# A fused convolution, MLP and top-1 expert kernel: the expert tiles as 89 of 256 tokens and 21 of 128, the first expert's weights queued ahead of its rows, and a second buffer for dispatched rows

## The chip, the cores and the metric

The kernel runs on one core of a Trainium2 chip. The metric is the device time of one launch in microseconds. Lower is better. The engines are called here as the profile calls them: PE multiplies matrices (its weight loads stand apart, as PEld), DVE and ACT do elementwise work, POOL does elementwise work and issues indirect DMAs, and SP issues nearly all other DMAs.

## The reference

Three blocks follow each other over 8 sequences of 3072 tokens of width 256, 24576 tokens in all: a long convolution by FFT, a dense MLP, and a layer of 8 experts in which each token goes to the one expert of its largest logit.

```python
def _attn_ref(x, filt_r, filt_i):
    X = np.fft.rfft(x, axis=1)
    F = (filt_r + 1j * filt_i)[None, :, :]
    return np.fft.irfft(X * F, n=x.shape[1], axis=1).astype(np.float32)

def _moe_ref(x, w_in, w_out):                      # 256 -> 2048 -> 256
    h = x @ w_in
    g = np.where(h > 0.0, h, np.exp(np.minimum(h, 0.0)) - 1.0)
    return (g @ w_out).astype(np.float32)

def _moe2_ref(x, w_gate, w1, w2):                  # 8 experts, 256 -> 1024 -> 256
    ...
    expert_idx = np.argmax(logits, axis=1)
    ...
    for e in range(E):
        mask = expert_idx == e
        ...
        h = np.maximum(x[mask] @ w1[e], 0.0)
        out[mask] = gate_w[mask, None] * (h @ w2[e])
```

## The kernel before

All matrix products stand for fp32: each operand is split into a high and a low f16 part, and each product is done in three passes (`PASSES`: high by high, high by low, low by high).

After a first stage (transforms of the first sequence, conversion of the weights) one long loop in `stream` runs 768 MLP steps. A step takes 256 tokens and 256 of the 2048 hidden units: 12 up matmuls of 256 columns (L1037), tanh and exp on ACT, two operations on DVE (L1044, L1045, they write `th`, of which there are 3 buffers), the split into `g` on ACT and POOL, and, `LAG` = 5 steps later, 12 down matmuls of 264 columns (L1066), 8 of which are the expert logits. All other work is strewn between the steps: the transforms of later sequences (L626 is one of their products), the conversion of the expert weights into a scratch tensor `wscr`, and the dispatch of tokens. A planner (`chain`) puts each small piece at a step where the engine loads allow it; within an engine the order so found is fixed.

**Dispatch.** `dispatch_steps` works on a group of three tiles of 512 tokens, 16 groups in all. After routing, the `rows` steps run once per tile. `s5` takes a `row` buffer, POOL writes two columns of it (L782, L784), ACT the high parts (a line of a helper, L167) and DVE the low parts (L170). Four `s6` steps then scatter 128 rows each by indirect DMA on POOL (L793) into the DRAM tensor `srt`, sorted by expert. All these scatters write one tensor, so each waits until the one before it has landed. There is one `row` buffer: the next tile's `s5` waits until the last scatter of the tile before has read it.

**Experts.** Behind the 768 steps and `LAG` more come the expert steps. Since the counts of the experts are known only at run time, there are `nmoe` = 103 tiles of 256 tokens, which is enough for any counts; which expert a tile takes and where its rows begin is read from tables (`table_steps`). The first table, of `EARLY` = 8 tiles, is made while the last group of tokens is still in the MLP; the second, of the other 95, when all counts are known. `pads` (L1164) then writes zero rows behind each expert's end, in POOL's order after 8 of the last group's 12 scatters. A tile is 8 steps. Each has 6 up matmuls of 256 columns (L1206), relu and split on ACT (L1209) and DVE (L1210), and, `XLAG` = 4 steps later, 6 down matmuls of 256 columns (L1225). After the last step of a tile ACT scales the two results into `eo` (L1230, 12 buffers) and POOL scatters them to the output (L1231).

**The queue of SP.** `expert_rows` loads a tile's rows by DMA transpose (`xT`, L1183, 8 buffers) and its gates and positions (`me`, L1185). `expert_weights` loads 1 MB of `w1` or `w2` (L1194) if the tile's expert differs from that of the tile two before; tiles use two weight buffers by turns. The first 8 tiles' rows are issued first, then the weights of tiles 0 and 1. From tile 5 on, the end of tile i issues the rows of tile i + `XROWS` = i + 3, so the rows of tile 8, the first that need the second table, all scatters and all pads, are issued when tile 5 ends, and SP waits there until these have landed.

In what follows w10, w20 are the two weight buffers of tile 0, w11, w21 those of tile 1.

Of the kernel before, what the change touches and what calls it, by code (L numbers as in the profile page):

```python
# [101 lines left out]
TE = 256  # L102
ROW = 516
# [6 lines left out]
EARLY = 8  # L110
# [5 lines left out]
class Kernel:  # L116
    def __init__(self, ctx, tc, a, nb):
# [4 lines left out]
        self.nmoe = self.ntok // TE + E - 1  # L122
# [241 lines left out]
    def expert_weight_steps(self, sb, psum_tile):  # L364
# [339 lines left out]
    def dispatch_steps(self, sb, psum_tile, g):  # L704
# [202 lines left out]
    def stream(self, ctx, fft, sf, sy, ps, psum_tile, yt):  # L907

        nc, tc, nb = self.nc, self.tc, self.nb
        with tc.tile_pool(name="mlp", bufs=1, reuse_waits="tile") as sb:  # L910
# [112 lines left out]
            for k in range(min(plan), nstep + LAG + 8 * self.nmoe + XLAG):  # L1023
# [55 lines left out]
    def table_steps(self, early):  # L1079


        nc, n = self.nc, EARLY if early else self.nmoe - EARLY
        st = {}

        def s1():
            sb = self.xb
            if early:
                self.kt = self.t(sb, [1, 2 * E + 2 * self.nmoe], F32, "kt", 1)
                nc.sync.dma_start(self.kt, self.a["k_tab"])
            else:  # L1090
# [5 lines left out]
        def s2():  # L1096
# [16 lines left out]
        def s4():  # L1113
            cf = st["cf"]
            nc.vector.tensor_scalar(out=cf[:, 3, :], in0=cf[:, 1, :], scalar1=-float(TE), scalar2=float(self.cap), op0=ALU.mult, op1=ALU.add)
            if early:
                self.done = d = self.t(self.xb, [1, E], F32, "done", 1)
                nc.vector.tensor_tensor(out=d, in0=cf[:, 1, :], in1=cf[:, 2, :], op=ALU.subtract)
                nc.vector.tensor_scalar(out=d, in0=d, scalar1=float(EARLY), scalar2=0.0, op0=ALU.add, op1=ALU.max)
                nc.vector.tensor_tensor(out=d, in0=d, in1=cf[:, 1, :], op=ALU.min)  # L1120
            else:
# [175 lines left out]
```

## Time and profile before

| | before |
|---|---|
| median of 3 runs | 3755.59 us (3749.76 to 3758.88) |
| the profiled execution | 3759.05 us |
| its span, first to last instruction | 3757.4 us |
| mean granted clock of TensorE in it | 0.971 |
| PE busy | 3515.3 us, 94% of the span |
| DVE, ACT, POOL busy | 2537.5, 2450.1, 1677.4 us |

The rows are read as follows. Times are microseconds from the start of the span. In the timeline a row is a run of like instructions: its start, its length, engine, line, operation, output<-input, shapes, count, and in brackets how long the engine stood idle before it and what ended that. "a*b" in a matmul is the size of the weights, "a x b" that of the moving data; the matmuls are pipelined, so the time between two starts tells the cost, and the printed lengths overlap. PEclk 1.00 is a granted clock of 2.4 GHz, half of it 1.2 GHz.

### The profile page before, as it was taken

How to read it: one execution, taken by the hardware profiler on the slowest of the kernel's cores; microseconds unless marked ns; L12 is line 12 of the kernel's file. 1: busy time of each engine (PE TensorE's matmuls, PEld its weight loads, DVE VectorE, ACT ScalarE, POOL GpSimd, SP SyncE). 2: the span in 40 equal slices, each digit the busy share in tenths (PEclk: the TensorE clock that was granted, in tenths of full speed). 3: DMA queues.
4: the chain of work that ended last, by engine and by line, in shares of the span. 5: the costliest groups of instructions: out<-in, count | busy, mean ns of one | idle time of the engine just before them, and what ended most of it. 6: DMA issues, size and time to landing. Idle time of an engine off the chain costs nothing. (4 is left out here: it accounts for less than half of the span.)

```text
span 3757.4 us, 83940 instructions
## 1 busy us (share of the span) xinstructions
PE 3515.3 (94%) x31644; PEld 3048.6 (81%) x31644; DVE 2537.5 (68%) x4684; ACT 2450.1 (65%) x4556; POOL 1677.4 (45%) x1554
## 2 busy tenths in 40 slices
PE   3599899999999999999999999999799999999998
PEld 1377788888888888788888888888688888888887
DVE  4788779979988987987997986766333333333332
ACT  2486788888788788788788788777233333333333
POOL 1434447646655655655664665555221111111111
PEclk7689999999999999999999999999899999999999
DMA  7725324334333433433433422101332332333231
GB/s 227 217 87 157 97 83 142 102 95 132 102 107 103 120 105 101 130 91 97 137 93 90 119 84 79 49 18 33 95 102 52 93 87 60 96 96 85 63 94 35
DMA packets 313610, 371.65 MB, mean 99 GB/s; under 512 B 162558, under 2 KB 236544, under 8 KB 307714
## 3 DMA queue, kind: packets, MB, share of 16 engines
q1 hardware_dynamic: 292226, 312.28, 30.6%
q0 software_dynamic: 19360, 52.67, 4.2%
q8 instruction: 248, 4.06, 0.5%
q10 hardware_dynamic: 1616, 1.32, 0.2%
q14 instruction: 160, 1.31, 0.1%
HBM read 404.01 MB, written 123.44 MB: 140 GB/s over the span
## 5 line engine op out<-in xcount | busy, mean ns | idle before, releaser
L1051 POOL TENSOR_TENSOR g<-th,g 128x512 f16<-128x512 f32 x768 | 899.0, 1171 | 878.4 <-ACT g L167 800.9
L1037 PE MATMUL up<-yh,w_in 128*128 128x256 f16 x9216 | 1147.0, 275 | 35.1 <-DVE th L1045 32.1
L1066 PE MATMUL dn<-w_out,g 128*128 128x264 f16 x9216 | 1153.9, 277 | 9.4 <-ACT x L1073 9.4
L1037 PEld LDWEIGHTS <-w_in 128*128 128x128 f16 x9216 | 902.7, 99 | 179.5 <-issue 46.7
L1066 PEld LDWEIGHTS <-g 128*128 128x128 f16 x9216 | 905.9, 98 | 145.0 <-issue 9.7
L1210 DVE SCALAR_TENSOR_TENSOR hh<-up,hh 128x256 f16<-128x256 f32 x824 | 349.6, 425 | 711.2 <-ACT hh L1209 689.9
L1209 ACT ACTIVATE hh<-up 128x256 f16<-128x256 f32 x824 | 316.1, 384 | 685.5 <-PE up L1206 648.3
L1044 DVE SCALAR_TENSOR_TENSOR th<-ex,yS,th 128x512 f32<-128x512 f32 x768 | 574.3, 748 | 232.7 <-ACT ex L1043 208.4
L1206 PE MATMUL up<-xT,w 128*128 128x256 f16 x4944 | 677.7, 274 | 26.0 <-DVE hh L1210 17.1
L1043 ACT ACTIVATE ex<-up,yS,yI 128x512 f32<-128x512 f32 x768 | 574.3, 748 | 152.7 <-DVE th L1044 150.8
L1042 ACT ACTIVATE th<-up,yI 128x512 f32<-128x512 f32 x768 | 524.8, 683 | 208.7 <-PE up L1037 175.9
L1045 DVE SCALAR_TENSOR_TENSOR th<-th,up 128x512 f32<-128x512 f32 x768 | 528.6, 688 | 87.0 <-DVE th L1044 2.8
L1231 POOL DMA_INDIRECT out<-eo,me x206 | 202.2, 982 | 829.3 <-ACT eo L1230 486.1
L1206 PEld LDWEIGHTS <-w 128*128 128x128 f16 x4944 | 485.3, 98 | 84.5 <-issue 17.5
L1225 PEld LDWEIGHTS <-hh 128*128 128x128 f16 x4944 | 485.0, 98 | 57.1
L167 ACT ACTIVATE g<-th 128x512 f16<-128x512 f32 x768 | 483.4, 629 | 11.1 <-DVE th L1045 2.5
L1225 PE MATMUL dn<-w,hh 128*128 128x256 f16 x2496 | 342.0, 274 | 0.0
L1225 PE MATMUL ff<-w,hh 128*128 128x256 f16 x2448 | 333.9, 273 | 0.0
L793 POOL DMA_INDIRECT srt<-row,pi x192 | 198.0, 1031 | 144.2 <-DMA srt<-row,pi 119.4
L560 POOL TENSOR_TENSOR t<-t,t 128x512 f32<-128x512 f32 x96 | 124.8, 1300 | 48.6 <-DVE t L554 35.3
L554 DVE SCALAR_TENSOR_TENSOR t<-ff,fs,ft 64x512 f32<-64x512 f32 (+1 forms) x186 | 130.8, 709 | 2.5
L579 PEld LDWEIGHTS <-e 128*128 128x128 f16 x648 | 66.5, 105 | 76.0 <-issue 35.2
(266 smaller groups left out, 2781.2 us busy)
## 6 DMA issues: line engine op xcount, KB each, us to landing
w<-wscr SPq DMA_DIRECT2D x103, 1024.5 KB
w<-wscr SPq DMA_DIRECT2D x103, 1024.0 KB
ft<-filt SPq DMA_DIRECT2D x96, 512.0 KB
at<-ascr SPq DMA_DIRECT2D x192, 128.0 KB
bscr<-bst SPq DMA_DIRECT2D x192, 128.0 KB
bt<-bscr SPq DMA_DIRECT2D x64, 384.0 KB
x<-x SPq DMA_DIRECT2D x84, 256.0 KB
x<-x SPq DMA_DIRECT2D x112, 192.0 KB
```

Source lines behind the costliest of these rows:

```text
L167: self.nc.scalar.activation(out, in_, AF.Copy, scale=scale)
L1037: nc.tensor.matmul(p[:, c * TH:(c + 1) * TH], self.w_in[:, w, d, ff:ff + 128], h[:, m, d, c0:c0 + TH], start=(i == 0), stop=(i == 5))
L1042: nc.scalar.activation(th, p, AF.Tanh, scale=I[:, 1:2])
L1043: nc.scalar.activation(e, p, AF.Exp, bias=S[:, 2:3], scale=I[:, 0:1])
L1044: nc.vector.scalar_tensor_tensor(out=th, in0=e, scalar=S[:, 1:2], in1=th, op0=ALU.add, op1=ALU.mult)
L1045: nc.vector.scalar_tensor_tensor(out=th, in0=th, scalar=0.0, in1=p, op0=ALU.min, op1=ALU.max)
L1051: nc.gpsimd.tensor_tensor(out=g[:, 1, :], in0=th, in1=g[:, 0, :], op=ALU.subtract)
L1066: nc.tensor.matmul(dn[s][:, 0:D + E], g[:, m, c * TH + s * 128:c * TH + s * 128 + 128], self.w_out[:, 2 * f + c, w, :], start=(f == 0 and ...
L1206: nc.tensor.matmul(p, w1[:, w0:w0 + 128], xT[:, 2 * m + d, :], start=(q == 0), stop=(q == 5))
L1209: nc.scalar.activation(h[:, 0, :], p, AF.Relu)
L1210: nc.vector.scalar_tensor_tensor(out=h[:, 1, :], in0=p, scalar=0.0, in1=h[:, 0, :], op0=ALU.max, op1=ALU.subtract)
L1225: nc.tensor.matmul(self.xd[s], h[:, m, s * 128:(s + 1) * 128], w2[:, w0:w0 + D], start=(f == 0 and q == 0), stop=(f == 7 and q == 2))
```

## The change

- **Tiles.** 89 full tiles of 256 tokens and 21 parts of 128 tokens take the place of 103 full tiles. The full tiles cover what is certain to fill them; a third table gives each part its expert and place. A part stands after about every fourth full tile, from the tenth on. It has 4 steps; each has two chunks of 6 up matmuls with 128 columns, the same work for ACT and DVE as before, and 6 down matmuls of 256 columns. Parts use a third pair of weight buffers, one `xP` and two `mP` buffers for their rows, and are loaded when the part before has ended.
- **Buffers.** `row` 1 to 2; `wst` 3 to 2 (raw weights in conversion, with two more of the MLP's raw blocks in `ft`), `eo` 12 to 6, `xT` and `me` 8 to 7 (`EARLY` 8 to 7, so tile 7 is now the first that needs the second table, and its rows are issued when tile 4 ends).
- **SP's queue.** The four weight loads of tiles 0 and 1 are issued first, then the rows of tiles 0 to 6.
- **Tables and pads.** Each table gets one or two more short steps; the pads come after all three tables.

In the changed kernel the lines are some 3 further down in the first part (row scatter L796, `th` L1047 and L1048), and in the expert part: rows L1207, `me` L1209, weights L1218, up L1236, down L1260, output L1266, pads L1181.

The diff, cut to its core:

```diff
-EARLY = 8
+EARLY = 7
...
-        self.nmoe = self.ntok // TE + E - 1
+
+        self.nmoe = -(-(self.ntok - E * (TE - 1)) // TE)
+        self.npart = (self.ntok + E * (TP - 1)) // TP - 2 * self.nmoe
...
-            t = self.t(sb, [128, 1024], F32, "wst", 3)
+            t = self.t(sb, [128, 1024], F32, "wst", 2)
...
-                st["ri", i] = ri = self.t(sb, [128, 4, ROW // 2], I32, "row", 1)
+                st["ri", i] = ri = self.t(sb, [128, 4, ROW // 2], I32, "row", 2)
...
-                    pool, tag, n = (sf, "ft", 2) if 3 <= c < 5 else (sb, "wst", 3)
+                    pool, tag, n = (sf, "ft", 2) if c % 4 > 1 else (sb, "wst", 2)
...
-            ke = chain(ke, self.table_steps(True), kd[last + 1] + 8)
-            ke = max(ke, ks[last] + 8) + 1
+            ke = chain(ke, self.table_steps(0), kd[last + 1] + 8)
+            ke = max(ke, ks[last] + 2) + 1
+            for i in range(2):
+                at(ke + i, lambda i=i: (self.expert_weights(0, i, 0), self.expert_weights(0, i, 1)), ZERO)
             for i in range(EARLY):
-                at(ke + i // 2, lambda i=i: self.expert_rows(i), ZERO)
-            for i in range(2):
-                at(ke + 5 + i, lambda i=i: (self.expert_weights(i, 0), self.expert_weights(i, 1)), ZERO)
-            assert ke + 6 < nstep + LAG
-            kt = chain(kd[ng - 1], self.table_steps(False))
+                at(ke + 2 + i // 2, lambda i=i: self.expert_rows(0, i), ZERO)
+            assert ke + 6 < nstep + LAG, (ke, nstep)
+            kt = chain(chain(kd[ng - 1], self.table_steps(1)), self.table_steps(2))
             at(kt, self.pads, ZERO)
...
+        nc, n = self.nc, (EARLY, self.nmoe - EARLY, self.npart)[kind]
...
+        def s4b():
+            cf = st["cf"]
+            d = self.t(self.xb, [1, E], F32, "done", 2)
+            nc.vector.tensor_tensor(out=d, in0=cf[:, 1, :], in1=cf[:, 2, :], op=ALU.subtract)
+            nc.vector.tensor_scalar(out=d, in0=d, scalar1=float(n), scalar2=0.0, op0=ALU.add, op1=ALU.max)
+            nc.vector.tensor_tensor(out=d, in0=d, in1=cf[:, 1, :], op=ALU.min)
+            if kind:
+                nc.vector.tensor_tensor(out=d, in0=d, in1=self.done, op=ALU.add)
+            self.done = d
...
-        big = 0.1 if early else 1.0
-        return [((c, 0.0, 0.0), 1, f) for c, f in ((0.2, s1), (0.8, s2), (1.0, s3), (0.7, s4), (2 * big, s5), (2 * big, s6), (0.8, s7))]
+            self.tab[kind] = tab
+
+        big = 1.0 if kind == 1 else 0.2
+        steps = [(0.4, s1), (0.8, s2), (0.8, s3), (0.8, s4)] + ([(0.5, s4b)] if kind < 2 else []) + [(2 * big, s5), (2 * big, s6), (0.8, s7), (0.7, s8)]
+        return [((c, 0.0, 0.0), 1, f) for c, f in steps]
...
-        self.w1 = [self.t(sb, [128, 4096], F16, f"w1{i}", 1) for i in range(2)]
-        self.w2 = [self.t(sb, [128, 4098], F16, f"w2{i}", 1) for i in range(2)]
+        self.w1 = [self.t(sb, [128, 4096], F16, f"w1{i}", 1) for i in range(3)]
+        self.w2 = [self.t(sb, [128, 4098], F16, f"w2{i}", 1) for i in range(3)]
...
+        at, m = {}, self.nmoe - EARLY
+        for h in range(self.npart):
+            at.setdefault(EARLY + (h + 1) * m // (self.npart + 1), []).append((1, h))
+        self.order = [v for i in range(self.nmoe) for v in [(0, i)] + at.get(i, [])]
+        self.xsteps = [(part, i, f) for part, i in self.order for f in range(4 if part else 8)]
...
+        xT = self.t(sb, [128, 4, n], F16, "xP" if part else "xT", 1 if part else EARLY)
+        nc.sync.dma_start_transpose(xT, self.srt[bass.ds(r, n), 0:D].bitcast(F16))
+        me = self.t(sb, [128, n // 128, 2], I32, "mP" if part else "me", 2 if part else EARLY)
...
-        self.nc.sync.dma_start(dst[i % 2], src[:, c0:c1], cond=(g > 0), cond_hint=False)
+        self.nc.sync.dma_start(dst[2 if part else i % 2], src[:, c0:c1], cond=(g > 0), cond_hint=False)
...
+            part, i, f = self.xsteps[k]
+            if not part and i == EARLY and f == 0:
+                self.expert_rows(1, 0)
+                self.expert_weights(1, 0, 0)
+                self.expert_weights(1, 0, 1)
+            w1, (xT, _) = self.w1[2 if part else i % 2], self.tile_x[part, i]
+            n, nf = (TP, 2) if part else (TE, 1)
             p = self.t(ps, [128, 512], F32, "up", 3)[:, 0:TE]
-            q = 0
-            for w, m in PASSES:
-                for d in range(2):
-                    w0 = w * 2048 + d * 1024 + f * 128
-                    nc.tensor.matmul(p, w1[:, w0:w0 + 128], xT[:, 2 * m + d, :], start=(q == 0), stop=(q == 5))
-                    q += 1
+            for c in range(nf):
+                q = 0
+                for w, m in PASSES:
+                    for d in range(2):
+                        w0 = w * 2048 + d * 1024 + (f * nf + c) * 128
+                        nc.tensor.matmul(p[:, c * n:(c + 1) * n], w1[:, w0:w0 + 128], xT[:, 2 * m + d, :], start=(q == 0), stop=(q == 5))
+                        q += 1
...
+            if f == 8 // nf - 1:
+                self.expert_weights(part, i + (1 if part else 2), 0)
...
+            for s in range(n // 128):
+                for c in range(nf):
+                    for q, (m, w) in enumerate(PASSES):
+                        w0 = w * 2048 + (f * nf + c) * D
+                        h0 = (s + c) * 128
+                        nc.tensor.matmul(self.xd[s], h[:, m, h0:h0 + 128], w2[:, w0:w0 + D], start=(f == 0 and c == 0 and q == 0), stop=(f == last and c == nf - 1 and q == 2))
...
-                    o = self.t(sb, [128, D], F32, "eo", 12)
+                for s in range(n // 128):
+                    o = self.t(sb, [128, D], F32, "eo", 6)
...
+                self.expert_weights(part, i + (1 if part else 2), 1)
+                if part:
+                    self.expert_rows(1, i + 1)
+                elif i + XROWS >= EARLY:
+                    self.expert_rows(0, i + XROWS)
```

On SP, the first loads of the expert stage (TENSOR_LOAD reads a table entry, ISA rows are register work). Before:

```order
L1089 DMA kt_36235<-k_tab 1x222 [waits DMAHW7_49]
L1175 TENSOR_LOAD tab_5422_36512 [waits DVE_49]
L1175 ISA x2
L1183 ISA
L1183 DMA_TRANSPOSE xT_36591<-srt 128x4x256 [waits DMAHW0_49,DMASW3_49]
L1185 ISA
L1185 DMA me_36593<-srt 128x2x2 [waits DMAHW1_49,PE_49]
L1175 TENSOR_LOAD tab_5422_36512
...
L1194 DMA w_4964_33056<-wscr 128x4096 [waits DMAHW0_49]
```

and in the changed kernel:

```order
L1198 TENSOR_LOAD tab_5432_36582 [waits DVE_49]
...
L1218 DMA w_4964_33056<-wscr 128x4096 [waits DMAHW5_49,DMAHW6_49,DMAHW0_49,PE_49]
...
L1218 DMA w_4967_33059<-wscr 128x4098 [waits DMAHW1_49]
...
L1218 DMA w_4965_33057<-wscr 128x4096
...
L1218 DMA w_4968_33060<-wscr 128x4098
...
L1207 DMA_TRANSPOSE xT_36810<-srt 128x4x256 [waits DMASW3_49]
...
L1209 DMA me_36812<-srt 128x2x2
```

The weights moved from behind the eight tiles' rows to ahead of them.

On DVE, the end of the first table (`tab`), between the operations on `th` that belong to the last MLP steps. Before:

```order
L1144 TENSOR_SCALAR tb_5413_36435<-tb_5413_36435 1x8
L1146 MEMSET tb_5413_36435 1x2
L1151 TENSOR_TENSOR tb_5413_36435<-tb_5413_36435 1x6 [waits DVE_49]
L1153 CAST tab_5422_36512<-tb_5413_36435 1x24 [waits DVE_49]
L1044 SCALAR_TENSOR_TENSOR th_36528<-ex_36527,yS_34129,th_36528 128x512 [waits Activation_49,Pool_49]
L1045 SCALAR_TENSOR_TENSOR th_36528<-th_36528,up_36514 128x512 [waits DVE_49,PE_49]
...
L1044 SCALAR_TENSOR_TENSOR th_36807<-ex_36806,yS_34129,th_36807 128x512 [waits Activation_49,Pool_49]
L1045 SCALAR_TENSOR_TENSOR th_36807<-th_36807,up_36793 128x512 [waits DVE_49,PE_49]
L1210 SCALAR_TENSOR_TENSOR hh_36975<-up_36968,hh_36975 128x256 [waits DMAHW6_49,Activation_49]
```

and in the changed kernel:

```order
L1165 MEMSET tb_5419_36471 1x2
L1167 TENSOR_TENSOR tb_5419_36471<-tb_5419_36471 1x5
L1169 CAST tab_5432_36582<-tb_5419_36471 1x21 [waits DVE_49]
L1047 SCALAR_TENSOR_TENSOR th_36598<-ex_36597,yS_34131,th_36598 128x512 [waits Activation_49,Pool_49]
L1048 SCALAR_TENSOR_TENSOR th_36598<-th_36598,up_36584 128x512 [waits DVE_49,PE_49]
...
L1047 SCALAR_TENSOR_TENSOR th_36781<-ex_36780,yS_34131,th_36781 128x512 [waits Activation_49,Pool_49]
L1048 SCALAR_TENSOR_TENSOR th_36781<-th_36781,up_36767 128x512 [waits DVE_49,PE_49]
L1240 SCALAR_TENSOR_TENSOR hh_36964<-up_36957,hh_36964 128x256 [waits DMAHW5_49,DMAHW4_49,Activation_49]
```

The table was followed by six pairs on `th` before the first expert operation (`hh`), and is now followed by four: it ends two MLP steps later.

On POOL, the rows of the last group (the first number after `row_` names the buffer's use; 37190, 37377 and 37614 are the three tiles before, 37179, 37366 and 37524 the same three after). Before:

```order
L793 DMA srt<-row_37190,pi_37128 200448x258 [waits DMASW0_49,DVE_49]
L782 TENSOR_TENSOR row_37377<-sm_37169,rp_5496_37147 128x4 [waits DMASW1_49]
L784 TENSOR_SCALAR row_37377<-idt 128x4
L793 DMA srt<-row_37377,pi_37128 200448x258 [waits DVE_49,Pool_49]
L1231 DMA out<-eo_37441,me_36606 24576x256 [waits DMASW5_49,Activation_49]
...
L793 DMA srt<-row_37377,pi_37128 200448x258 [waits DMASW6_49,DVE_49]
...
L1164 DMA srt<-k_pad 16x4128 [waits DMASW7_49]
...
L782 TENSOR_TENSOR row_37614<-sm_37169,rp_5496_37147 128x4
...
L793 DMA srt<-row_37614,pi_37128 200448x258 [waits DMASW7_49,DVE_49,Pool_49]
```

and in the changed kernel:

```order
L796 DMA srt<-row_37179,pi_37117 200448x258 [waits DMASW0_49,DVE_49]
L785 TENSOR_TENSOR row_37366<-sm_37158,rp_5496_37136 128x4
L787 TENSOR_SCALAR row_37366<-idt 128x4
L796 DMA srt<-row_37366,pi_37117 200448x258 [waits DMASW1_49,DVE_49,Pool_49]
L1266 DMA out<-eo_37431,me_36825 24576x256 [waits DMASW5_49,Activation_49]
...
L796 DMA srt<-row_37366,pi_37117 200448x258 [waits DMASW6_49,DVE_49]
L785 TENSOR_TENSOR row_37524<-sm_37158,rp_5496_37136 128x4
L787 TENSOR_SCALAR row_37524<-idt 128x4
L796 DMA srt<-row_37524,pi_37117 200448x258 [waits DMASW7_49,DVE_49,Pool_49]
...
L796 DMA srt<-row_37524,pi_37117 200448x258 [waits DMASW2_49,DVE_49]
...
L1181 DMA srt<-k_pad 16x4128 [waits DMASW5_49]
```

The second tile's columns no longer wait for a scatter, and the pads moved from between the second and the third tile to behind the third.

## Rows read from the trace of the kernel before

**Rows 1.** The page, engines: busy time, share of the span, instructions.
```profile
PE 3515.3 (94%) x31644; PEld 3048.6 (81%) x31644; DVE 2537.5 (68%) x4684; ACT 2450.1 (65%) x4556; POOL 1677.4 (45%) x1554
```
**Rows 2.** Busy time by stretch: main loop, transition, expert stage, first loads (columns first).
```profile
core 0: us, PE busy (x) PEld busy (x) DVE busy (x) ACT busy (x) POOL busy (x), PEclk, DMA share, GB/s
200.00:2632.00 2432.00, 2333.96 (x21262) 2017.51 (x21263) 2028.74 (x3483) 1972.86 (x3388) 1394.74 (x1271) 0.99 0.34 98
2642.00:2757.00 115.00, 97.69 (x837) 84.74 (x838) 48.39 (x156) 37.86 (x100) 30.48 (x39) 0.91 0.27 81
2757.00:3740.00 983.00, 983.00 (x9007) 881.07 (x9006) 331.82 (x844) 362.07 (x939) 186.06 (x190) 1.00 0.32 80
...
2642.00:2646.00 4.00, 3.91 (x23) 2.96 (x24) 1.99 (x5) 1.07 (x3) 0.00 (x0) 0.62 0.97 367
```
**Rows 3.** Timeline of PE: a full expert tile's steps; then a transform beside MLP matmuls.
```profile
2710.41 0.82 PE L1206 MATMUL up<-xT,w 128*128 128x256 f16 x6
...
2711.72 0.82 PE L1206 MATMUL up<-xT,w 128*128 128x256 f16 x6
...
1349.40 0.68 PE L626 MATMUL ff<-c,bt 96*128 96x96 f16 x12
1349.91 1.48 PE L1037 MATMUL up<-yh,w_in 128*128 128x256 f16 x12
```
**Rows 4.** The page, groups: weight loads of the expert's up matmuls.
```profile
L1206 PEld LDWEIGHTS <-w 128*128 128x128 f16 x4944 | 485.3, 98 | 84.5 <-issue 17.5
```
**Rows 5.** Timeline of PE: its waits in the MLP loop; the last row a step without one.
```profile
2308.18 2.72 PE L1037 MATMUL up<-yh,w_in 128*128 128x256 f16 x12 [6.21 <-DVE th L1045]
...
2442.86 4.91 PE L1066 MATMUL dn<-w_out,g 128*128 128x264 f16 x24 [5.36 <-ACT x L1073]
...
2576.92 4.45 PE L1066 MATMUL dn<-w_out,g 128*128 128x264 f16 x24 [4.03 <-ACT x L1073]
...
2599.78 2.86 PE L1066 MATMUL dn<-w_out,g 128*128 128x264 f16 x24
```
**Rows 6.** Timeline of ACT, writing rows, and of POOL, scattering them, around these waits.
```profile
2304.11 0.91 ACT L167 ACTIVATE row<-x,rs 128x256 f16<-128x256 f32 x2 [8.83 <-DMA srt<-row,pi]
...
2439.87 0.91 ACT L167 ACTIVATE row<-x,rs 128x256 f16<-128x256 f32 x2 [6.70 <-DMA srt<-row,pi]
...
2573.93 0.91 ACT L167 ACTIVATE row<-x,rs 128x256 f16<-128x256 f32 x2 [3.86 <-DMA srt<-row,pi]
...
2300.95 0.99 POOL L793 DMA_INDIRECT srt<-row,pi  x1 [6.16 <-DMA srt<-row,pi]
```
**Rows 7.** Timeline of PE: the end of the MLP and the first expert tiles.
```profile
2625.07 8.26 PE L1066 MATMUL dn<-w_out,g 128*128 128x264 f16 x72
2642.09 4.88 PE L1206 MATMUL up<-xT,w 128*128 128x256 f16 x30 [8.76 <-DMA w<-wscr]
...
2677.81 1.44 PE L1206 MATMUL up<-xT,w 128*128 128x256 f16 x6 [10.16 <-DVE hh L1210]
...
2695.10 1.44 PE L1206 MATMUL up<-xT,w 128*128 128x256 f16 x6 [6.95 <-DVE hh L1210]
```
**Rows 8.** Timeline of DVE (MLP steps and the table's end) and of SP (loads).
```profile
2610.81 0.75 DVE L1044 SCALAR_TENSOR_TENSOR th<-ex,yS,th 128x512 f32<-128x512 f32 x1 [0.60 <-ACT ex L1043]
...
2612.87 0.17 DVE L1153 CAST tab<-tb 1x24 int32<-1x24 f32 x1
2613.47 0.75 DVE L1044 SCALAR_TENSOR_TENSOR th<-ex,yS,th 128x512 f32<-128x512 f32 x1 [0.43 <-ACT ex L1043]
...
2614.08 1.35 SPq L1183 DMA_TRANSPOSE xT<-srt  x1
...
2637.03 4.09 SPq L1194 DMA_DIRECT2D w<-wscr  x3
...
2733.96 1.34 SPq L1183 DMA_TRANSPOSE xT<-srt  x1
```
**Rows 9.** Timeline of POOL: the last group's scatters and the pads; the page, landing of pads.
```profile
2662.81 0.97 POOL L793 DMA_INDIRECT srt<-row,pi  x1 [0.30 <-issue]
...
2677.80 1.27 POOL L793 DMA_INDIRECT srt<-row,pi  x1 [1.58 <-DVE hh L1210]
...
2715.09 0.49 POOL L1164 DMA_DIRECT2D srt<-k_pad  x1 [2.52 <-DMA srt<-k_pad]
...
2731.36 0.97 POOL L793 DMA_INDIRECT srt<-row,pi  x1 [0.31 <-issue]
...
srt<-k_pad POOLq DMA_DIRECT2D x8, 258.0 KB, 2.9
```

More of the change, by code (lines that the diff above doesn't have):

```diff
@@ L102 @@
 TE = 256
+TP = TE // 2
 ROW = 516
@@ L1022, in stream @@
             ev, gh = {}, {}
-            for k in range(min(plan), nstep + LAG + 8 * self.nmoe + XLAG):
+            for k in range(min(plan), nstep + LAG + 8 * self.nmoe + 4 * self.npart + XLAG):
                 if k >= nstep + LAG:
@@ L1114, in s4 @@
             cf = st["cf"]
[L1115 to L1121, printed above, removed]
+            nc.vector.tensor_scalar(out=cf[:, 3, :], in0=cf[:, 1, :], scalar1=-float(TE if kind < 2 else TP), scalar2=float(self.cap), op0=ALU.mult, op1=ALU.add)
+            if kind:
                 d = self.done
@@ L1175, in entry, with expert_rows @@
+        for h in range(self.npart):
+            at.setdefault(EARLY + (h + 1) * m // (self.npart + 1), []).append((1, h))
+        self.order = [v for i in range(self.nmoe) for v in [(0, i)] + at.get(i, [])]
+        self.xsteps = [(part, i, f) for part, i in self.order for f in range(4 if part else 8)]
+    def entry(self, row, part, i, top):
+        tab, j = (self.tab[2], i) if part else (self.tab[0], i) if i < EARLY else (self.tab[1], i - EARLY)
         return self.nc.sync.value_load(tab[0:1, row, j:j + 1], min_val=0, max_val=top)
-    def expert_rows(self, i):
+    def expert_rows(self, part, i):
@@ L1178, in expert_rows @@
         nc, sb = self.nc, self.xb
-        if i >= self.nmoe:
+        if i >= (self.npart if part else self.nmoe):
             return
-        r = self.entry(1, i, self.rmax)
-        xT = self.t(sb, [128, 4, TE], F16, "xT", EARLY)
-        nc.sync.dma_start_transpose(xT, self.srt[bass.ds(r, TE), 0:D].bitcast(F16))
-        me = self.t(sb, [128, 2, 2], I32, "me", EARLY)
-        nc.sync.dma_start(me, self.srt[bass.ds(r, TE), D:D + 2].rearrange("(a p) f -> p a f", p=128))
-        self.tile_x[i] = (xT, me)
@@ L1188, in expert_weights @@
-    def expert_weights(self, i, w):
-        if i >= self.nmoe:
+        n = TP if part else TE
+        r = self.entry(1, part, i, self.rmax + TE - n)
+        xT = self.t(sb, [128, 4, n], F16, "xP" if part else "xT", 1 if part else EARLY)
+        nc.sync.dma_start_transpose(xT, self.srt[bass.ds(r, n), 0:D].bitcast(F16))
+        me = self.t(sb, [128, n // 128, 2], I32, "mP" if part else "me", 2 if part else EARLY)
+        nc.sync.dma_start(me, self.srt[bass.ds(r, n), D:D + 2].rearrange("(a p) f -> p a f", p=128))
@@ L1190, in expert_weights @@
+        self.tile_x[part, i] = (xT, me)
+    def expert_weights(self, part, i, w):
+        if i >= (self.npart if part else self.nmoe):
             return
[L1191 removed]
+        e, g = self.entry(0, part, i, E - 1), self.entry(2, part, i, 1)
         src = self.wscr[bass.ds(e, 1)].rearrange("a p f -> p (a f)")
         dst, c0, c1 = ((self.w1, 0, 4096), (self.w2, 4096, 8194))[w]
[L1194 removed]
+        self.nc.sync.dma_start(dst[2 if part else i % 2], src[:, c0:c1], cond=(g > 0), cond_hint=False)
@@ L1211, in expert_step @@
             self.hs[k] = h
-            if f == 7:
-                self.expert_weights(i + 2, 0)
+            if f == 8 // nf - 1:
+                self.expert_weights(part, i + (1 if part else 2), 0)
         if k >= XLAG:
-            i, f = divmod(k - XLAG, 8)
-            w2, (_, me) = self.w2[i % 2], self.tile_x[i]
+            part, i, f = self.xsteps[k - XLAG]
+            w2, (_, me) = self.w2[2 if part else i % 2], self.tile_x[part, i]
+            n, nf = (TP, 2) if part else (TE, 1)
             if f == 0:
-                self.xd = [self.t(ps, [128, 512], F32, ("dn", "ff")[i % 2], 2)[:, 0:D] for _ in range(2)]
-                self.cm = self.t(sb, [128, 2, 1], F32, "cm", 2)
+                t = self.order.index((part, i))
+                self.xd = [self.t(ps, [128, 512], F32, ("dn", "ff")[t % 2], 2)[:, 0:D] for _ in range(n // 128)]
+                self.cm = self.t(sb, [128, n // 128, 1], F32, "cmP" if part else "cm", 2)
                 self.mul(self.cm, me.bitcast(F32)[:, :, 0:1], w2[:, 4096:4098].bitcast(F32))
             h = self.hs.pop(k - XLAG)
-            for s in range(2):
-                for q, (m, w) in enumerate(PASSES):
-                    w0 = w * 2048 + f * D
-                    nc.tensor.matmul(self.xd[s], h[:, m, s * 128:(s + 1) * 128], w2[:, w0:w0 + D], start=(f == 0 and q == 0), stop=(f == 7 and q == 2))
-            if f == 7:
+            last = 8 // nf - 1
+            for s in range(n // 128):
[4 more added lines that the diff above has]
+                        nc.tensor.matmul(self.xd[s], h[:, m, h0:h0 + 128], w2[:, w0:w0 + D], start=(f == 0 and c == 0 and q == 0), stop=(f == last and c == nf - 1 and q == 2))
+            if f == last:
                 mi = me.bitcast(U32)
-                for s in range(2):
-                    o = self.t(sb, [128, D], F32, "eo", 12)
+                for s in range(n // 128):
+                    o = self.t(sb, [128, D], F32, "eo", 6)
                     nc.scalar.activation(o, self.xd[s], AF.Copy, scale=self.cm[:, s, :])
```

58 lines of the change are left out of this document (27 added, 31 removed).

## The prediction

> **What bounds the kernel now.** I read the engines' busy time first: PE is busy 94% of the span, the others 68% or less [rows 1]. Since that is an average, the stretches come next [rows 2]. In the expert stage from 2757 us on PE is busy 983.00 of 983.00 us at the full clock, with DVE, ACT and DMA at about a third: there each removed matmul is worth its own length. In the 115 us of transition before it PE is idle for 17.3 us. In the MLP loop it is idle for 98 of 2432 us. So I then read PE's timeline for what ended its waits: in the loop those with rows of the dispatch behind them [rows 5, 6], and those around the first expert tiles [rows 7].
>
> The profiled execution took 3759.05 us, 3.5 more than the median of the three runs (3755.59) and 1.7 more than its span. I sum against the execution and take 3.5 off at the end.
>
> **The tiles.** Full tile: one step is 2711.72 - 2710.41 = 1.31 us for 12 matmuls of 256 columns, so 0.109 us each, and 8 steps are 10.48 us [rows 3]. 14 full tiles go: -146.7 us. A part has 48 up matmuls of 128 columns and 24 down matmuls of 256. The trace has no f16 matmul of 128 columns. The nearest row is the transform's 12 matmuls of 96 columns, each with weights of its own: 1349.91 - 1349.40 = 0.51 us, 42.5 ns each [rows 3]. Between 96 columns at 42.5 and 256 at 109 ns a straight line gives 55.8 ns at 128. The bounds: half the price of 256 columns, 54.6 ns, below; above, the 98 ns that one weight load is shown as lasting [rows 4], if 128 columns were too short to hide it. I take 55.8, since 42.5 ns was reached with even shorter matmuls. A part is then 48 x 0.0558 + 24 x 0.109 = 5.30 us, and 21 are 111.3 us. Net **-35.4 us** (-36.6 at 54.6 ns, +7.1 at 98 ns). ACT and DVE have the same work per step as before, in steps of 5.30 / 4 = 1.32 us.
>
> On this point the Trainium skill speaks against the change ("TensorE: Matmul & The Clock Gate", section "Back-to-back issue gap"): a sustained stream of weight load and matmul pairs has 81 ns of spacing at 128 columns, and the shorter isolated gap undercounts. By that, as an estimate, a part would be 6.5 us and the net -10 us. The 42.5 ns at 96 columns are against it, though they come from runs of 12 between other matmuls.
>
> A part's weights go to a third pair of buffers and are asked for when the part before ends, some four full tiles or 40 us ahead, its rows likewise. Three weight loads take SP's queue 4.09 us [rows 8], and the stage moves only 80 GB/s where 367 were reached [rows 2]. I cost these loads at 0; the cover are those four tiles. Without it a part would wait about 3 us for its rows (landing after issue is 2.9 us for the pads, the nearest [rows 9]).
>
> **Two row buffers, in the loop.** With one buffer ACT must wait for the scatters of the tile before: 8.83, 6.70 and 3.86 us in front of three of these writes, and PE then runs dry for 6.21, 5.36 and 4.03 us [rows 5, 6], 15.6 in all; no other group shows such a wait of PE. Behind each, PE restarts at the half clock: 12 matmuls of 256 columns last 2.72 us and 24 of 264 last 4.91 and 4.45 where 2.86 is normal [rows 5], so some 1.25 + 2.05 + 1.6 = 4.9 us more. Together 20.5. In the changed order the second tile's row waits only for scatters of the group before, long landed; the third tile's row still waits for the first's scatters, which have a whole tile's time. One doubt: at 2300.95 POOL itself waited 6.16 us for a slow scatter [rows 6], and that wait stays, though fewer instructions of ACT stand behind it. I take **-18 us**; bounds -9 (the first wait stays and half of the others) and -20.5.
>
> **The transition.** All times are in the clock of before. PE ends the MLP at 2625.07 + 8.26 = 2633.3, and the first expert matmul waits until 2642.09 for weights [rows 7]. Before, the rows of eight tiles went first, from 2614.08 on, and the weights followed at 2637.03 [rows 8]. In the changed order the first table ends two MLP steps later; a step is 2613.47 - 2610.81 = 2.66 us [rows 8]. So the first weight load is issued at about 2614.1 + 5.3, say 2620. The four are 4.2 MB, at 367 GB/s 11.4 us, so landed by 2632 to 2633, with the first rows behind them at 2633 to 2635. The expert stage starts at about 2635, 7 us earlier.
>
> Not all of that stays. The rows of the first tile of the second table need all 12 scatters of the last group and 8 pads, one after another on POOL, each behind the landing of the one before. Before, the scatters began at 2662.81, and SP could issue these rows at 2733.96 [rows 8, 9], that is 20.7 and 91.9 us after the first expert matmul. That chain is not shorter now: the same 20 transfers, without bubbles of some 1.7 us where it waited for rows (1.58 of them at 2677.80 [rows 9]) and without 1.5 us of half-clock steps ahead of them. So issue at about 2635 + 89 = 2724, rows landed 3 us later, 2727. Before, tile 8 was the first that needed it and began at 2747.1 (step 4 of tile 4 is the one at 2710.41 [rows 3], and 28 steps of 1.31 follow): covered. Now it is **tile 7**. The two waits of 10.16 and 6.95 us that the single row buffer caused [rows 7] are gone, so PE has done seven tiles at 2635 + 7 x 10.48 less the 2.6 that the first four steps lack, near 2706. It waits there for about 21 us. That is where those stalls go: they are not removed but collected in one wait. With 2.3 us of half clock behind it, tile 8 begins at 2727 + 10.5 + 2.3 = 2739.8 and not 2747.1: **-7.3 us**. Bounds: 0, if the weights land no earlier than before, and -12, if the chain loses more bubbles than I count.
>
> **The rest**, each at 0: the row buffer's price in `wst` (one raw load in the first stage is issued some 11 us later, its data is wanted after that; up to +2), the extra table steps (DVE is busy a third in that stage [rows 2]), 6 `eo` buffers (a tile frees two in 10.48 us, a landing takes 3), and the end of the kernel, where a full tile stands as before.
>
> **Sum.** -35.4 - 18 - 7.3 = -60.7, so 3759.05 - 60.7 = 3698.4, less 3.5: **3695 us**.
>
> **Rivals.**
> 1. *Short matmuls paced by the weight loads.* 128 columns cost 98 ns [rows 4]: +7.1 in place of -35.4, so 3737. Half of the way there, 77 ns, gives 1008 x 0.021 = 21 us more than forecast, 3716. For it: loads and matmuls of the expert stage are paired one to one, and PEld is busy 90% of it [rows 2]. Against: 42.5 ns at 96 columns. Chance 0.10 for all of that stretch. The Trainium skill's rule above lies in it; by its 81 ns the time would be 3720, an estimate.
> 2. *The row buffer's gain comes late or not.* The waits of the loop are only delayed to the third tile's row or to POOL's chain, and the transition gives nothing: 9 to 20 us less gain, 3704 to 3715. For it: the chain of scatters is serial, and one slow landing was seen. Chance 0.16.
> 3. *Parts wait for their own loads*, one row buffer `xP` being too few or SP being held at a full tile's rows: 3 us for each of 21, 63 us, and nothing is gained: 3758. Against: 40 us of cover. Chance 0.05.
> 4. *Slower: the load of the next weights doesn't overlap so short a matmul.* A matmul then costs 98 + 56 = 154 ns, a part 10.0 us, 21 of them 210: the term becomes +63, and the time 3794. It turns slower when 128 columns cost more than 55.8 + 60.7 / 1.008 = 116 ns. No row shows such a case. Chance 0.04.
>
> **How the numbers follow.** The forecast has 0.65. Its own ends are -36.6 - 20.5 - 12 and -35.4 - 9 - 0 + 2, that is 3686 to 3713; the range must take in rival 2 and rival 1 up to 82 ns (1008 x 0.026 = 26 us), so 3682 to 3722, the low end 4 us wider for the scatter of the runs. A measurement of this kernel can tell some 0.3%, 11 us, from no change. Faster by more: forecast, rival 1 and rival 2, 0.91. Within it: rival 3, 0.05. Slower: rival 4, 0.04.
>
> **What would show it.** The tiles: in the timeline of PE a run of 12 up matmuls with 128 columns that starts 0.67 us before the down matmuls behind it, and 5.3 us per part with no idle time; 98 ns each would show as 1.18. The row buffers: no wait of PE over 3 us with `x` or `th` behind it in the loop, and no wait of ACT for `srt` at the second tile's row. The transition: weights issued near 2602 (2620 less the loop's 18), the first expert matmul near 2617, and one wait of about 21 us in front of tile 7, ended by its rows, with the pads last on POOL before it. If that wait is absent, my chain is too slow; if it is over 30, the pads behind three tables cost more than counted. The prediction would be wrong above all by the price of a 128-column matmul (10 ns are 10 us), then by a chain that starts later than 21 us after the first expert matmul.

## The result

The changed kernel takes 3701.17 us (3695.86 to 3705.39, 4 runs) where the kernel before took 3755.24 in the same series: a ratio of 0.9848, 95% interval 0.983 to 0.9865, or 54 us less. The profiled execution took 3698.49 us, its span is 3696.8. Predicted were 3695 and a range of 3682 to 3722.

**The profile after.** Busy time by stretch, as in [rows 2]:

```profile
core 0: us, PE busy (x) PEld busy (x) DVE busy (x) ACT busy (x) POOL busy (x), PEclk, DMA share, GB/s
200.00:2612.00 2412.00, 2318.41 (x21267) 2008.80 (x21264) 2040.40 (x3481) 1972.21 (x3387) 1392.26 (x1270) 1.00 0.35 100
2622.00:2737.00 115.00, 91.63 (x822) 80.89 (x821) 49.10 (x179) 36.72 (x97) 32.59 (x41) 0.91 0.32 83
2737.00:3680.00 943.00, 943.00 (x9133) 851.04 (x9132) 319.10 (x821) 348.02 (x900) 177.98 (x181) 1.00 0.39 97
```

PE is still busy for all of the expert stage. In these windows, which both begin behind the wait for the first expert matmul, the transition is idler than before (23.4 us against 17.3). PE's timeline, from the end of the MLP to the end of the kernel, with one part (against [rows 3, 7]):

```profile
2603.16 8.26 PE L1069 MATMUL dn<-w_out,g 128*128 128x264 f16 x72
2613.74 5.10 PE L1236 MATMUL up<-xT,w 128*128 128x256 f16 x30 [2.31 <-DMA xT<-srt]
...
2649.21 0.81 PE L1236 MATMUL up<-xT,w 128*128 128x256 f16 x6 [1.82 <-DVE hh L1240]
...
2710.09 1.46 PE L1236 MATMUL up<-xT,w 128*128 128x256 f16 x6 [21.42 <-DMA w<-wscr]
...
2722.21 0.82 PE L1236 MATMUL up<-xT,w 128*128 128x256 f16 x6
...
2754.97 0.83 PE L1236 MATMUL up<-xP,w 128*128 128x128 f16 x12
2755.64 0.82 PE L1260 MATMUL dn<-w,hh 128*128 128x256 f16 x6
2756.30 0.83 PE L1236 MATMUL up<-xP,w 128*128 128x128 f16 x12
...
3681.73 3.44 PE L1260 MATMUL ff<-w,hh 128*128 128x256 f16 x30
```

The MLP ends at 2603.16 + 8.26 = 2611.42 (2633.33 before), the first expert matmul waits 2.31 us and no longer 8.76, one wait of 21.42 us has taken the place of 10.16 and 6.95 (with the 1.82 us, PE's waits sum to 25.55 us, where they summed to 25.87), and the row at 2722.21 is the first of tile 8 (2747.1 before). SP and POOL in the same stretch (against [rows 8, 9]):

```profile
2598.41 6.02 SPq L1218 DMA_DIRECT2D w<-wscr  x4
2605.17 2.52 SPq L1207 DMA_TRANSPOSE xT<-srt  x1
...
2706.48 1.29 SPq L1207 DMA_TRANSPOSE xT<-srt  x1
...
2709.99 1.74 SPq L1218 DMA_DIRECT2D w<-wscr  x2
```

```profile
2634.70 0.97 POOL L796 DMA_INDIRECT srt<-row,pi  x1 [0.31 <-DVE cf L1114]
...
2661.50 0.95 POOL L796 DMA_INDIRECT srt<-row,pi  x1 [2.41 <-DVE hh L1240]
...
2666.49 1.06 POOL L796 DMA_INDIRECT srt<-row,pi  x1 [3.62 <-DMA srt<-row,pi]
...
2703.62 0.49 POOL L1181 DMA_DIRECT2D srt<-k_pad  x1 [2.60 <-DMA srt<-k_pad]
```

The weights are issued first; the scatters begin 21 us after the first expert matmul, the last pad is issued at 2703.62, and SP can issue tile 7's rows at 2706.48. PE starts 3.6 us later, when SP has also come to the weight entries that stand behind these rows in its queue.

### The profile page after: what moved, and what is told of

The parts are those of the page before. It is cut to its first block, busy times and chain, and to the rows that moved or that the text cites. A ratio compares the mean times of both kernels' runs of the same rounds, so it can differ in the third digit from the quotient of the medians.

```text
span 3696.8 us, 84477 instructions
## 1 busy us (share of the span) xinstructions
PE 3457.0 (94%) x31812; PEld 3010.7 (81%) x31812; DVE 2543.4 (69%) x4697; ACT 2438.3 (66%) x4521; POOL 1671.9 (45%) x1547
## 5 line engine op out<-in xcount | busy, mean ns | idle before, releaser
L1240 DVE SCALAR_TENSOR_TENSOR hh<-up,hh 128x256 f16<-128x256 f32 x796 | 337.3, 424 | 696.7 <-ACT hh L1239 696.6
L1239 ACT ACTIVATE hh<-up 128x256 f16<-128x256 f32 x796 | 304.7, 383 | 671.6 <-PE up L1236 654.3
L1047 DVE SCALAR_TENSOR_TENSOR th<-ex,yS,th 128x512 f32<-128x512 f32 x768 | 573.7, 747 | 219.6 <-ACT ex L1046 196.6
L1236 PE MATMUL up<-xT,w 128*128 128x256 f16 x4272 | 584.7, 273 | 25.7 <-DMA w<-wscr 21.4
L1048 DVE SCALAR_TENSOR_TENSOR th<-th,up 128x512 f32<-128x512 f32 x768 | 528.5, 688 | 87.3 <-DVE th L1047 4.2
L1236 PEld LDWEIGHTS <-w 128*128 128x128 f16 x5280 | 482.3, 98 | 78.2 <-DMA w<-wscr 21.7
L1266 POOL DMA_INDIRECT out<-eo,me x178 | 175.5, 986 | 736.6 <-ACT eo L1265 395.6
L1260 PEld LDWEIGHTS <-hh 128*128 128x128 f16 x4776 | 464.1, 98 | 52.5
L1260 PE MATMUL dn<-w,hh 128*128 128x256 f16 x2400 | 328.0, 273 | 0.0
L1260 PE MATMUL ff<-w,hh 128*128 128x256 f16 x2376 | 323.4, 273 | 0.0
L796 POOL DMA_INDIRECT srt<-row,pi x192 | 197.4, 1028 | 138.0 <-DMA srt<-row,pi 87.3
```

What stands on the lines that cost most here:

```text
L1047: nc.vector.scalar_tensor_tensor(out=th, in0=e, scalar=S[:, 1:2], in1=th, op0=ALU.add, op1=ALU.mult)
L1048: nc.vector.scalar_tensor_tensor(out=th, in0=th, scalar=0.0, in1=p, op0=ALU.min, op1=ALU.max)
L1236: nc.tensor.matmul(p[:, c * n:(c + 1) * n], w1[:, w0:w0 + 128], xT[:, 2 * m + d, :], start=(q == 0), stop=(q == 5))
L1239: nc.scalar.activation(h[:, 0, :], p, AF.Relu)
L1240: nc.vector.scalar_tensor_tensor(out=h[:, 1, :], in0=p, scalar=0.0, in1=h[:, 0, :], op0=ALU.max, op1=ALU.subtract)
L1260: nc.tensor.matmul(self.xd[s], h[:, m, h0:h0 + 128], w2[:, w0:w0 + D], start=(f == 0 and c == 0 and q == 0), stop=(f == last and c == nf - ...
```

## The experiments

For each profiled execution two figures are used beside the timed ratio: when the MLP ends, and how long PE then takes to its last matmul (the end of the last row of its timeline). The second needs no comparison between runs of the loop. For the kernel before the last row is

```profile
3742.03 3.44 PE L1225 MATMUL dn<-w,hh 128*128 128x256 f16 x30
```

so 3745.47 - 2633.33 = 1112.1 us; in the changed kernel 3685.17 - 2611.42 = 1073.8.

| kernel | us, median | ratio to before, 95% interval | MLP ends | from there to PE's end |
|---|---|---|---|---|
| before | 3755 to 3764 | | 2633.3 | 1112.1 |
| changed | 3701.17 | 0.9848 [0.983, 0.9865] | 2611.4 | 1073.8 |
| changed, again (e10) | 3705.26 | 0.9853 [0.9828, 0.9879] | 2617.9 | 1074.0 |
| one row buffer (e1) | 3720.41 | 0.9892 [0.9876, 0.9909] | 2631.8 | 1074.6 |
| rows first (e2) | 3720.27 | 0.9888 [0.9869, 0.9908] | 2622.1 | 1085.8 |
| before, two row buffers, 6 eo (e3) | 3743.75 | 0.9953 [0.9939, 0.9967] | 2614.3 | 1115.0 |
| before, two row buffers, 12 eo (e7) | 3734.62 | 0.9914 [0.989, 0.9938] | 2622.1 | 1105.5 |
| full tiles only (e6) | 3738.72 | 0.995 [0.993, 0.9969] | 2604.6 | 1111.7 |
| 8 early tiles, 4 eo (e4) | 3709.06 | 0.9862 [0.9846, 0.9879] | 2621.5 | 1078.0 |
| 8 early tiles, 6 eo (e8) | 3702.52 | 0.9834 [0.9814, 0.9854] | 2620.6 | 1067.2 |
| two pads a tile (e5) | 3698.61 | 0.9849 [0.9831, 0.9868] | 2610.9 | 1068.6 |
| one pad a tile (e9) | 3682.54 | 0.9776 [0.9756, 0.9797] | 2617.4 | 1051.9 |
| parts late, pads as changed (e11) | 3702.95 | 0.9843 [0.9819, 0.9867] | 2614.7 | 1074.1 |

**One row buffer (e1).**

```diff
-                st["ri", i] = ri = self.t(sb, [128, 4, ROW // 2], I32, "row", 2)
+                st["ri", i] = ri = self.t(sb, [128, 4, ROW // 2], I32, "row", 1)
```

> The changed kernel with one row buffer again. If the second buffer is what took the waits out of the MLP loop, three waits of PE of about 15.6 us with 4.9 us of half clock behind them come back, and ACT waits 4 to 9 us for srt in front of them: the loop is 20 to 22 us longer. At the transition the two waits of some 10 and 7 us come back too, but the wait in front of tile 7 (21.4 us now) shrinks by as much, so that it adds only some 2 us for bubbles of POOL's chain: 3701 + 23 = 3724 us. Rival: the loop's gain comes from the new order of the other pieces, not from the buffer: then PE shows no wait over 3 us in the loop, and the time stays within 5 us of 3701.

The waits came back where they had been [rows 5], and at the transition two waits with a small rest in front of tile 7:

```profile
2306.08 2.72 PE L1040 MATMUL up<-yh,w_in 128*128 128x256 f16 x12 [6.04 <-DVE th L1048]
...
2440.54 5.30 PE L1069 MATMUL dn<-w_out,g 128*128 128x264 f16 x24 [5.51 <-ACT x L1076]
...
2575.30 4.50 PE L1069 MATMUL dn<-w_out,g 128*128 128x264 f16 x24 [4.26 <-ACT x L1076]
...
2668.86 1.44 PE L1236 MATMUL up<-xT,w 128*128 128x256 f16 x6 [9.98 <-DVE hh L1240]
...
2686.49 1.44 PE L1236 MATMUL up<-xT,w 128*128 128x256 f16 x6 [6.99 <-DVE hh L1240]
...
2731.01 0.83 PE L1236 MATMUL up<-xT,w 128*128 128x256 f16 x6 [2.71 <-DMA w<-wscr]
```

In the changed kernel they are gone. The lists of waits in the loop (200 to 2604 us: total, times, longest) have, in the kernel before,

```profile
PE up L1037 <- DVE th L1045: 32.1, 21, 6.2
PE dn L1066 <- ACT x L1073: 9.4, 2, 5.4
ACT row L167 <- DMA srt<-row,pi: 32.4, 15, 8.8
```

and in the changed one, of these three, only

```profile
PE up L1040 <- DVE th L1048: 27.4, 21, 1.9
```

The ratio of e1 is 0.0044 above that of the changed kernel, some 17 us. So the second buffer is what empties the loop of these waits, and it is worth 0.8 us behind the loop (1074.6 against 1073.8): there the stalls are only collected in front of tile 7.

**Rows first (e2).** The seven `expert_rows` are put back ahead of the four weight loads.

> The changed kernel with the rows of tiles 0 to 6 issued ahead of the first four weight loads, as before. The seven rows take SP some 19 us, so the first weights are issued near 2617 of the trace and the first expert matmul comes near 2622, not 2613.7. Theory: the last group's scatters are tied to the expert steps, so the whole chain up to tile 7 shifts along, and the time is 8 us longer, 3709 us, with the wait in front of tile 7 still about 21 us. Rival: the chain of scatters and pads has its own clock, the wait in front of tile 7 shrinks by the 8 us, and the time stays at 3701 us.

The first expert matmul came 11.6 us after the MLP's end and not 2.3, and the wait in front of tile 7 stayed at 22.45 us. The theory holds, with 12.0 us in place of 8: the scatters move with the expert steps (the first of them begins 21.5 us after the first expert matmul, 21.0 in the changed kernel).

**The row buffer in the kernel before (e3, e7).** `row` 2 and `wst` 2, with 6 `eo` buffers and with 12.

> The kernel before with two row buffers, and with the space for them taken as in the change (wst 2, eo 6); 103 full tiles, rows first, 8 early tiles. Theory: the loop gains 20 to 22 us; at the transition the two waits behind the row buffer go, but tile 8 then waits some 11 us for its rows, which the same serial chain of 12 scatters and 8 pads releases: net 4 to 7 us there. 3755 - 27 = 3728 us. Rival (a gain that is only delayed): the first wait of the loop stays, and the transition gives nothing, 9 us in all: 3746 us.

> The kernel before with two row buffers and wst 2, but with its 12 eo buffers kept. Theory: what ate the transition's gain with 6 of them was ACT, held 18 us for an eo buffer because POOL's output scatters stand behind the pads; with 12 that wait is gone, tile 8 waits only for its rows (some 9 us), and from the end of the MLP to the end of PE's work it takes some 1104 us, where the kernel before took 1112 and the one with 6 buffers 1115. With the loop's gain of about 18 us: 26 us less than the kernel before. Rival: the second row buffer is worth nothing at the transition; then 1112 us or more.

With 6 the transition lost 3 us where a gain was expected. ACT's waits of that kernel, from 2600 to 2760 us (total, times, longest), name the cause:

```profile
ACT eo L1230 <- DMA out<-eo,me: 20.7, 2, 18.0
```

POOL's output scatters stand behind the pads, the `eo` buffers stay full, ACT is held, and PE with it, for 18.31 us. With 12 buffers PE's one long wait is 10.08 us in front of tile 8, ended as in the changed kernel, and 6.6 us are gained (1112.1 to 1105.5).

**Full tiles only (e6).** 103 full tiles, no parts, two tables.

> The changed kernel with 103 full tiles and no parts, all else as changed (7 early tiles, weights first, two row buffers; two tables). Theory: 14 x 10.48 - 21 x 5.30 = 35.4 us longer, 3736.5 us, with the same wait of about 21 us in front of tile 7. Rival: parts disturb their neighbours by loads and small DMAs, or help beyond their matmuls: then the difference is off 35 by more than 5 us.

1111.7 - 1073.8 = 37.9 us. The parts alone can be read behind the transition: from DVE's first operation on `hh` of tile 9 to PE's end it takes 986.6 us in all four traces with 103 full tiles (before, e3, e6, e7) and 951.2 us in the changed kernel, e1, e2, e4, e8, e10 and e11, which is 35.4 us. The excess of 2.5 lies in the transition: the pads there come ahead of the last two scatters, ACT again waits for `eo` (20.5 us), and PE waits 20.80 us at the last step of tile 6 and 1.22 us in front of tile 7, with half-clock steps behind both.

**One more early tile (e4, e8).** `EARLY` 8, first with `eo` cut to 4, then with 6 and one `hh` buffer less.

> The changed kernel with 8 early tiles, eo cut from 6 to 4 buffers for the space. Theory: the wait in front of tile 7 is the serial chain of 12 scatters and 8 pads on POOL, which is released about 93 us after the first expert matmul whatever PE does; with one more tile of 10.48 us to do meanwhile, the wait stands in front of tile 8 and lasts 21.4 - 10.5 = 11 us: 3701 - 10.5 = 3690.5 us. Rival: the trace names a weight load as what ended that wait; if a load as such is what PE waits for, the wait keeps its 21 us and the time stays at 3701 us.

> The changed kernel with 8 early tiles and its 6 eo buffers; the space comes from one hh buffer less (5) and one shared table of work. Theory: the wait stands in front of tile 8, lasts some 11 us, and from the end of the MLP to the end of PE's work it takes 1063 us, where the changed kernel took 1074: 10 us less in all. Rival: 6 eo buffers are already too few for one more tile ahead of the pads, ACT waits for one, and less than 5 us are gained.

Neither theory's number came. ACT's waits for `eo`, in the first and in the second kernel:

```profile
ACT eo L1265 <- DMA out<-eo,me: 28.1, 4, 18.1
```

```profile
ACT eo L1265 <- DMA out<-eo,me: 16.5, 2, 13.4
```

PE's long waits follow ACT. In the first kernel they stand at the last steps of tiles 5 and 6, in the second at the last step of tile 7 (the row by itself), none in front of tile 8:

```profile
2692.01 0.94 PE L1236 MATMUL up<-xT,w 128*128 128x256 f16 x6 [4.79 <-DVE hh L1240]
...
2722.76 1.44 PE L1236 MATMUL up<-xT,w 128*128 128x256 f16 x6 [18.44 <-DVE hh L1240]
```

```profile
2721.08 1.44 PE L1236 MATMUL up<-xT,w 128*128 128x256 f16 x6 [14.03 <-DVE hh L1240]
```

So the output buffers run out before the rows of tile 8 are missed: 4.2 us lost with 4 of them, 6.6 gained with 6, not 10.5. That the wait for the rows moves to tile 8 and lasts some 11 us is not shown by these two; e7, with 8 early tiles and 12 `eo`, has it there, with 10.08 us.

**The pads out of the chain (e5, e9, e11).** Only parts read padded rows. In the first kernel two pads stand behind the rows of each of tiles 7 to 10, in the second

```diff
-            at(kt, self.pads, ZERO)
...
                     self.expert_rows(0, i + XROWS)
+                    e = i + XROWS - EARLY - 1
+                    if 0 <= e < E:
+                        self.pads(e, e + 1)
```

with the parts from tile 19 on; the third has only the later parts.

> The changed kernel with the 8 pads taken out of the chain: two pads each are issued behind the rows of tiles 7, 8, 9 and 10 (only parts read padded rows), and parts stand from tile 14 on. Theory: rows of tile 7 are then issued right behind the last scatter, near 2682 of the trace, some 25 us earlier than now, and land before PE is through with tile 6 (2688.7): the wait of 21.4 us goes, with the 1.6 us of half clock behind it. 3701 - 23 = 3678 us, provided that each pair of pads (two landings of 3.1 us, and the rows' own of 3) fits into a tile of 10.48 us. Rival: the pads only move, and each tile from 8 on waits for its pair: 4 waits of 3 to 6 us, 3690 us or more.

> The changed kernel with one pad behind the rows of each of tiles 8 to 15, and the parts from tile 19 on. With two pads a tile, POOL's work of a tile (two output scatters and two pads at some 3.2 us) took more than the tile's 10.48 us, and the weight loads stood in SP's queue behind rows that waited for pads. With one it is some 9.6 us. Theory: no wait over 3 us is left behind the first expert matmul, and from the end of the MLP to the end of PE's work it takes some 1050 us (1074 in the changed kernel, 1069 with two pads a tile): 23 us less than the changed kernel, some 3678 us. Rival: rows, output scatters and pads hold each other up with one pad as well, and 1065 us or more remain.

> The changed kernel with its parts from tile 19 on and their first loads at tile 14, as in the kernel with one pad a tile, but with the pads where the change has them. If that kernel gains by its pads, this one is as fast as the changed kernel, within 5 us, with the wait of about 21 us in front of tile 7. Rival: the later parts are what gains; then this one is some 20 us faster than the changed kernel too.

With two pads a tile 5.2 us of the 23 came. PE's timeline:

```profile
2702.23 0.83 PE L1235 MATMUL up<-xT,w 128*128 128x256 f16 x6 [3.23 <-DMA w<-wscr]
...
2738.35 1.44 PE L1259 MATMUL dn<-w,hh 128*128 128x256 f16 x6 [7.42 <-DMA w<-wscr]
```

Weight loads were late, standing in SP's queue behind rows that waited for pads, which POOL could only fit between output scatters. With one pad a tile PE's waits from 2560 us on are

```profile
PE up L1235 <- DMA xT<-srt: 3.6, 2, 2.4
PE up L1235 <- DVE hh L1239: 3.1, 2, 2.5
PE up L1039 <- DVE th L1047: 0.5, 1, 0.5
```

and 21.9 us are gone, 1051.9 against 1073.8. The later parts alone change nothing (1074.1). The kernel with one pad a tile beats both the changed kernel and the one before: 3682.54 us beside 3764.04 for the kernel before.

**The changed kernel again (e10).**

> The changed kernel itself once more, beside the next run on the same chip. It should stand 54 to 57 us below the kernel before, with the wait of about 21 us in front of tile 7. It tells how far the end of the MLP moves between executions of one program: 2611 us in the first trace, where kernels with the same loop had 2605 to 2622.

Behind the MLP the two executions agree to 0.3 us; the end of the MLP itself differs by 6.5 us.

## Why the prediction was right, and where it was off

| step | predicted | the two traces |
|---|---|---|
| tiles (start of tile 8 to PE's end) | -35.4 | 998.4 to 963.0: -35.4 |
| row buffers in the loop (end of the MLP) | -18 | 2633.3 to 2611.4: -21.9 |
| transition (MLP's end to tile 8) | -7.3 | 113.8 to 110.8: -3.0 |
| the rest | 0 | -0.3 |
| sum | -60.7 | -60.6 |

**The tiles: right to the tenth.** 12 matmuls of 128 columns take 2755.64 - 2754.97 = 0.67 us, 55.8 ns each, as the straight line between 96 and 256 columns gave. The term itself is 35.4 us (e6). So rivals 1 and 4 are out: the loads of 98 ns overlap the matmuls. The Trainium skill's 81 ns for 128 columns ("TensorE: Matmul & The Clock Gate", section "Back-to-back issue gap") is not what this stream of pairs shows; the measurement decides. Rival 3 is out too: no part waited.

**The sum: its agreement to 0.1 us is luck.** The transition gave 4.3 us less than forecast and the loop of this one pair of traces 3.9 more, and the two cancel.

**The loop: the mechanism is shown, and the size is close.** e1 brings the three waits back. The one pair of traces gives 21.9 us; but over the 11 traces with two buffers the MLP ends between 2604.6 and 2622.1, 2616.1 on the mean, over the two with one at 2633.3 and 2631.8: 16.4 us. The three waits all stand in the last 128 of the 768 steps. These begin, with the 641st pair on `th`, in the kernel before and in the changed one at

```profile
2256.11 0.75 DVE L1044 SCALAR_TENSOR_TENSOR th<-ex,yS,th 128x512 f32<-128x512 f32 x1
```

```profile
2252.94 0.75 DVE L1047 SCALAR_TENSOR_TENSOR th<-ex,yS,th 128x512 f32<-128x512 f32 x1
```

From there to the MLP's end the two traces with one buffer take 377.2 and 378.0 us, the 11 with two 358.5 to 361.5, 360.2 on the mean: the buffer is worth 17.4 us, where I took 18. The other 3.2 us of the pair (2256.11 to 2252.94) lie ahead of that, where step 641 begins anywhere from 2244.4 to 2262.1 us with two buffers, and at 2256.1 and 2253.8 with one; the buffer is not seen to change anything there. One wait there was missed in the prediction: PE waits 3.38 us for `th` at 1584.85 in the kernel before. It is not the buffer's, since e4, e6 and e7, with two, show one of 3.70 to 4.19 us at 1579 to 1589, while e1 has none over 3 us there, nor has the changed kernel. What moves these first steps by up to 17 us between executions is open. It is also why medians give 54 us and the two traces 60.6: the changed kernel's trace lies 2.7 us below its median, that of the kernel before 3.8 above.

**The transition: the order of events right, the size off by 4.3 us.** The expert stage started 6.5 us earlier (7 predicted), and the stalls were collected in front of tile 7 (21.42 us, 21 predicted). The step that failed is "that chain is not shorter now ... without bubbles of some 1.7 us ... and without 1.5 us of half-clock steps ahead of them". From the first scatter to the rows' issue the chain took 2706.48 - 2634.70 = 71.8 us; before it was 2733.96 - 2662.81 = 71.2 [rows 8, 9]. One bubble went (1.58 us before) and another came (3.62 us at 2666.49, also seen in other kernels with two buffers; why the scatter ahead of it is slow to land is open). The half-clock steps ahead of the scatters did not go either: the first 30 expert matmuls take 2618.68 - 2613.74 = 4.94 us, 4.71 before, where 3.28 are normal. So the rows were issued 92.7 us after the first expert matmul, not 89, which is most of the 4.3. The wait matched only because PE, too, came 4 us later than reckoned, by these half-clock steps and by a wait of 1.82 us at tile 3; that is luck.

The 3.0 us that were gained are hardly idle time, since PE's waits sum to 25.87 us before and 25.55 after. They are half clock. The rows at which the full clock is back are, before,

```profile
2646.80 0.82 PE L1225 MATMUL dn<-w,hh 128*128 128x256 f16 x6
...
2682.75 0.82 PE L1206 MATMUL up<-xT,w 128*128 128x256 f16 x6
...
2699.93 0.82 PE L1206 MATMUL up<-xT,w 128*128 128x256 f16 x6
```

and after

```profile
2618.68 0.82 PE L1260 MATMUL dn<-w,hh 128*128 128x256 f16 x6
...
2713.69 0.82 PE L1260 MATMUL dn<-w,hh 128*128 128x256 f16 x6
```

With 6 matmuls in 0.655 us as the normal price, the three restarts of before (2642.09, 2677.81, 2695.10) cost 1.4, 2.3 and 2.2 us, the two of after (2613.74, 2710.09) 1.7 and 1.6: 2.7 us less. So rival 2 came near about the transition, whose stalls were moved and not removed, and was wrong about the loop.

**The rest.** "6 eo buffers" at 0 was right for this change, but by a narrow margin that I had not seen: I priced them by the landing of a scatter, not by the 25 us of pads ahead of them on POOL. With the pads in their old place (e3), or with one tile more (e8), they are the bound.

## What to carry to other kernels

Price a new matmul size from two sizes in the trace: start to start, not by the length printed for a weight load. Where several stalls lie ahead of one serial chain, removing them only collects them in front of whoever needs the chain's end; ask what in the chain that consumer really reads. Here it needed no pads, and taking them out gave 22 us, provided that they were spread so thinly that neither POOL nor SP's queue was blocked by them.

## What was not expected of the hardware

One program's loop of 768 steps ended at 2611.4 and at 2617.9 us in two executions, and kernels with the same loop spread over 17 us, while the 1074 us behind it repeat to 0.3 us. The spread arises ahead of step 641; in the kernels with two `row` buffers the last 128 steps agree to 3 us.

The other is the clock after a wait of PE. After the wait of 21.42 us the granted clock was lower for the first steps (0.61 of full speed on the mean from 2710.0 to 2714.4 us; the first 6 matmuls start to start in 1.26 us and not 0.65), which cost 1.6 us. After the wait of 2.71 us (e1) the first 6 ran at full speed, but the half clock came 1.3 us later and cost 1.7 us:

```profile
2732.36 1.49 PE L1236 MATMUL up<-xT,w 128*128 128x256 f16 x6
```

The length of the wait alone does not decide it: after 2.31 us at the MLP's end the changed kernel's clock fell (0.65 on the mean of the next 4.94 us), after 1.82 us there, and after 2.37 and 2.52 us in the kernel with one pad a tile, it stayed at 1.00.
